# Sliding-window attention followed by a gated feed-forward: engine orders from a list scheduler on a model of the chip, PSUM banks given per stage, copies on either engine

## The chip, the cores and the metric

One core of a Trainium2 chip runs the whole program. The metric is device time in microseconds (us) of one execution. The kernel before takes 366.1 us. A comparison within 1% comes from runs in five rounds against the kernel before on the same chip.

Five engines run unsynchronized and in order, each its own list of instructions: TensorE (PE; PEld is its weight load), VectorE (DVE), ScalarE (ACT), GpSimd (POOL, which here issues the loads) and SyncE (SP, which issues the stores). They wait for one another by semaphores.

## The reference

Batch 8, 8 heads, sequence 576, head dimension 64. Attention with a causal window of 128 and a distance bias for each head, then a feed-forward over all 4608 tokens:

```python
scores = (q @ k.T) / 8 - slope[h] * abs(i - j)       # kept where 0 <= i - j < 128
attn   = exp(scores - max) / sum
x      = (attn @ v) transposed to (B*S, H*D)         # 4608 x 512
h      = x @ w_in                                    # 512 -> 2048, "GEMM 1"
g      = h * cos(h)
out    = g @ w_out                                   # 2048 -> 512, "GEMM 2"
```

## The kernel before

A small recorder keeps the instructions in the order in which the program is written, engine by engine, and derives the semaphore waits from what each operation reads and writes. So the order of every engine is the author's. PSUM is the memory that TensorE writes its results to; it is used here in eight banks. PSUM banks are keys such as `("B", 4)`: an operation that uses a bank waits for the one that used it last.

The feed-forward works in nine chunks of 512 tokens. Chunk `c` runs its GEMM 1 with the q/k transposes of batch `c+1` in between, then its GEMM 2 as filler between the pieces of attention `c+1`:

```python
def qk_transposes(banks, engs):         # 8 steps: pl in 0,1; q, k; columns (0,5) and (5,9)
    ...                                 # a step: 10 or 8 transposes into one bank, then
    ...                                 # one copy out, engs[n % 2] = "dve", "act"

def moe1(c, fc):                        # GEMM 1, one block of 128 hidden columns
    bank = HB[fc % 6]                   # banks 0..5
    ...                                 # 4 matmuls 128x512, cos on ACT, h*cos(h) on DVE

def moe2_steps(c):                      # GEMM 2: 4 outputs of 16 matmuls, banks 6 and 7
    ...                                 # copied out by DVE, stored by SP

def attention(b, fill, plan):           # units: ("t", None) = tail, then (pair, half)
    lead, part, last = plan
    take(lead)                          # lead matmuls of GEMM 2
    for j in range(2):
        scores(b, us[j], j); exps(b, us[j], j)
    mask(b, us[0])
    for j in range(n + 2):
        take(part[0] if j < n else last)
        if 2 <= j:      x_back(b, us[j - 2], j - 2, "act")
        if j + 2 < n:   scores(b, us[j + 2], j + 2); exps(b, us[j + 2], j + 2)
        if j < n:       take(part[1]); pv(b, us[j], j)
        if j + 1 < n:   mask(b, us[j + 1])
        if j < n:       norm(b, us[j], j)

for c in range(NCH):                    # ... c < 7:
    steps = iter(qk_transposes([6, 7], ["dve", "act"]))
    for fc in range(16):
        moe1(c, fc)
        if fc % 2 == 1:
            next(steps)()
    ...                                 # loads of batch c + 2
    attention(c + 1, moe2_steps(c), (8, (2, 3), 3))
```

A unit of attention is a pair of heads with one half of the first 512 positions; the tail is the last 64 positions, for all heads. PV is `attn @ v`. `take(n)` issues n filler matmuls of GEMM 2, and `x_back` transposes a finished unit into x.

TensorE uses its array in three ways. GEMMs, PV and most x transposes take it whole; the scores and the tail's x transposes use 64 rows at a time; the q/k transposes write 64 columns at a time. A change between these is called a tiling switch below.

The softmax here doesn't subtract the row's maximum and nothing guards it: scores larger than these inputs give would overflow.

Of the kernel before, what the change touches and what calls it, by code (L numbers as in the profile page):

```python
# [20 lines left out]
XA = 5 * CH  # L21
VW = 66


class Op:
    __slots__ = ("eng", "fn", "proc", "idx", "waits", "clock", "need", "val", "dma")


class Recorder:
# [3 lines left out]
    ENG = ("pe", "act", "dve", "pool", "sp")  # L33

    def __init__(self, nc, ctx):
        self.nc, self.ctx = nc, ctx
        self.handle = {"pe": nc.tensor, "act": nc.scalar, "dve": nc.vector,
                       "pool": nc.gpsimd, "sp": nc.sync}
        self.ops = {e: [] for e in self.ENG}
        self.writer, self.readers = {}, {}  # L40
        self.known = {e: {} for e in self.ENG}
        self.count = {}
        self.last = {}
        self.byproc = {}

    def _need(self, deps, d):
        if d is None:
            return
        cur = deps.get(d.proc)
        if cur is None or cur.idx < d.idx:  # L50
            deps[d.proc] = d

    def op(self, eng, fn, r=(), w=(), dma=None):
        o = Op()
        o.eng, o.fn, o.dma, o.need = eng, fn, dma, False
        raw, order = {}, {}
        for k in r:
            self._need(raw, self.writer.get(k))
        for k in w:
            self._need(order, self.writer.get(k))  # L60
            for d in self.readers.get(k, {}).values():
                if d.proc != eng or eng == "pool":
                    self._need(order, d)
        if dma is not None:
            self._need(order, self.last.get(("dma", dma)))
        known = self.known[eng]
        deps = dict(raw)
        for d in order.values():
            if d.proc == eng and eng == "pe":
                continue  # L70
            self._need(deps, d)
        if eng == "pe":
            deps.pop("pe", None)
        o.waits = []
        for p, d in sorted(deps.items(), key=lambda kv: str(kv[0])):
            if known.get(p, -1) >= d.idx:
                continue
            d.need = True
            o.waits.append(d)
        for d in o.waits:  # L80
            for p, i in d.clock.items():
                if known.get(p, -1) < i:
                    known[p] = i
            if known.get(d.proc, -1) < d.idx:
                known[d.proc] = d.idx
        o.proc = ("dma", dma) if dma is not None else eng
        o.idx = self.count.get(o.proc, 0)
        self.count[o.proc] = o.idx + 1
        o.clock = dict(known)
        self.last[o.proc] = o  # L90
        self.byproc.setdefault(o.proc, []).append(o)
        self.ops[eng].append(o)
        for k in r:
            self.readers.setdefault(k, {})[o.proc] = o
        for k in w:
            self.writer[k] = o
            self.readers[k] = {}
        return o

    def finish(self, final=()):  # L100
        nc, ctx = self.nc, self.ctx
        sems = {}
        for p, ops in self.byproc.items():
            name = p if isinstance(p, str) else f"d_{p[1]}"
            sems[p] = ctx.enter_context(nc.semaphore(f"s_{name}"))
            n = 0
            for o in ops:
                if o.dma is not None:
                    n += 16 * (len(o.fn) if isinstance(o.fn, list) else 1)
                elif o.need:  # L110
                    n += 1
                o.val = n
        block = ctx.enter_context(nc.Block())

        def run(e):
            h = self.handle[e]
            for o in self.ops[e]:
                for d in o.waits:
                    h.wait_ge(sems[d.proc], d.val)
                if o.dma is not None:  # L120
                    for f in (o.fn if isinstance(o.fn, list) else [o.fn]):
                        f(h).then_inc(sems[o.proc], 16)
                else:
                    ins = o.fn(h)
                    if o.need:
                        ins.then_inc(sems[e], 1)
            if e == "sp":
                for p in final:
                    h.wait_ge(sems[p], self.byproc[p][-1].val)
# [21 lines left out]

def bass_alibi_sliding__then__act_gcu_kernel(
# [8 lines left out]
    with ExitStack() as ctx:  # L161
# [3 lines left out]
        R = Recorder(nc, ctx)  # L165
# [12 lines left out]
        NP = 3  # L178
# [15 lines left out]
        HB = [0, 1, 2, 3, 4, 5]  # L194
# [12 lines left out]
        def load_qk(which, src, b):  # L207
            fns = []
            for g in range(2):
                fns.append(lambda e, g=g: e.dma_start(  # L210
                    qB[which][64 * g:64 * g + 64, :, :],
                    src[b, 4 * g:4 * g + 4, :, :].rearrange("h (s j) d -> s h (j d)", j=9)))
            op("pool", fns, w=[("qB", which)], dma=f"ld{which}")

        def load_v(b, order=range(NBLK)):
            for t in order:
                rows = 128 if t < 4 else 64
                op("pool", lambda e, t=t, rows=rows: e.dma_start(  # L218
                    vp[b % 2][0:rows, t, :, 0:64],
                    v[b, :, 128 * t:128 * t + rows, :].rearrange("h p d -> p h d")),  # L220
                   r=[("vinit", b % 2)], w=[("v", b % 2, t)], dma=f"ldv{b % 2}{t}")

        def load_w_in(u):
            op("pool", lambda e: e.dma_start(
                w_in[:, :, 512 * u:512 * u + 512],
                moe_w_in[:, 512 * u:512 * u + 512].rearrange("(k p) c -> p k c", p=128)),
               w=[("wi", u)], dma=f"wi{u}")

        def load_w_out(u):
            op("pool", lambda e: e.dma_start(  # L230
                w_out[:, 4 * u:4 * u + 4, :],
                moe_w_out[512 * u:512 * u + 512, :].rearrange("(f p) j -> p f j", p=128)),
               w=[("wo", u)], dma=f"wo{u}")


        def constants():
# [4 lines left out]
               w=["dif"] + sel)  # L241
            op("pool", lambda e: e.affine_select(
                dif[:, 0, :], dif[:, 0, :], pattern=[[-1, 128]], compare_op=ALU.is_ge,
                fill=-1.0e6, base=-1, channel_multiplier=1), r=["dif"], w=["dif"] + sel)
            op("pool", lambda e: e.affine_select(
                dif[:, 1, :], dif[:, 1, :], pattern=[[1, 128]], compare_op=ALU.is_ge,
                fill=-1.0e6, base=0, channel_multiplier=-1), r=["dif"], w=["dif"] + sel)
# [13 lines left out]
        def masks():  # L261
            for h in range(H):
# [3 lines left out]
                    ACTF.Exp, scale=slopes[h]), r=["dif"], w=[("EM", h)])  # L266
            for x in range(2):
# [3 lines left out]
                   r=[("EM", h) for h in range(x, H, 2)], w=["EMt"])  # L271


        def qk_transposes(banks, engs):

            out_ = []
            n = 0
            for pl in range(2):
                for which in ("q", "k"):
                    for (j0, j1) in ((0, 5), (5, 9)):  # L280
                        def step(pl=pl, which=which, j0=j0, j1=j1, n=n):
                            bank = banks[n % len(banks)]
                            nj = j1 - j0
                            dst = ps[:, bank, :].bitcast(BF16)[:, 0:nj * 128]

                            def tp(e):
                                ins = None
                                for j in range(j0, j1):
                                    for x in range(2):
                                        ins = e.transpose(  # L290
                                            dst[64 * x:64 * x + 64,
                                                128 * (j - j0):128 * (j - j0) + 128],
                                            qB[which][:, 2 * pl + x, 64 * j:64 * j + 64],
                                            ident[:, :])
                                return ins
                            op("pe", tp, r=[("qB", which), "ident"], w=[("B", bank)])
                            o = tr[which][:, :].rearrange("p (g l t) -> p g l t", g=2, l=2)[
                                :, :, pl, 0:576].rearrange("p g (s j) -> p g s j", j=9)[
                                :, :, :, j0:j1]
                            i = dst.rearrange("p (j g s) -> p g s j", j=nj, g=2)  # L300
                            key = ("tr", which, pl, j0)
                            if engs[n % len(engs)] == "act":
                                op("act", lambda e: e.activation(o, i, ACTF.Copy),  # L303
                                   w=[("B", bank), key])
                            else:
                                op("dve", lambda e: e.tensor_copy(o, i), w=[("B", bank), key])  # L306
                        out_.append(step)
                        n += 1
            return out_
# [7 lines left out]
        def units(b):  # L317
            if b == 0:
                return [(pr, G) for G in range(2) for pr in (0, 2, 1, 3)] + [("t", None)]
            return [("t", None)] + [(pr, G) for pr in range(NPAIR) for G in range(2)]  # L320

        def scores(b, u, n):
            slot = n % 2
            banks = [2 * slot, 2 * slot + 1]

            def f(e):
                ins = None
                if u[0] == "t":
# [314 lines left out]
```

## Time and profile before

| | before |
|---|---|
| time, median | 366.1 us |
| span of the profiled run | 365.3 us |
| TensorE busy | 93% |
| tiling switches on TensorE, in the order | 241 |
| length of a steady stage (one chunk and one attention) | 39.13 us |

From the page of the kernel before: busy time by engine; then the span in 40 slices, where each digit is the busy share, or the granted share of TensorE's clock, in tenths; then the chain of work that ended last, by engine.

```profile
PE 341.4 (93%) x2912; PEld 164.6 (45%) x2912; DVE 233.1 (64%) x446; ACT 234.5 (64%) x352; POOL 61.3 (17%) x89
PE   0688999999999999999999999999999999999996
PEclk9955999999999999999999999999999999999999
PE 79%; ACT 10%; DVE 6%; DMA 2%; issue 1%; POOL 1%; ACTq 0%; DVEq 0%; POOLq 0%
```

TensorE is nearly always busy from the fourth slice on, and the other engines have a third of their time free. But "busy" hides things: the time shown for a matmul is its latency (380 ns on average for L528), and matmuls overlap (they start 216 ns apart). The starts tell more. The timeline of TensorE, first two lines of the head, then part of one stage (start us, us from first start to last end, engine, line, operation, tiles, shapes, how many):

```profile
8.76 1.17 PE L290 MATMUL ps<-ident,qrows 128*64 128x128 bf16 x18 [8.76 <-DMA qrows<-in_q_dram]
...
30.62 3.57 PE L505 MATMUL ps<-xT,w_inb 128*128 128x512 bf16 x8 [0.24 <-ACT xT L487]
...
150.04 1.89 PE L505 MATMUL ps<-xT,w_inb 128*128 128x512 bf16 x8
151.86 0.47 PE L290 MATMUL ps<-ident,qrows 128*64 128x128 bf16 x10
152.26 1.90 PE L505 MATMUL ps<-xT,w_inb 128*128 128x512 bf16 x8
154.09 0.41 PE L290 MATMUL ps<-ident,qrows 128*64 128x128 bf16 x8
...
169.50 0.41 PE L333 MATMUL ps<-qt,kt 64*128 64x64 bf16 x16
169.74 0.33 PE L342 MATMUL ps<-qt,kt 64*128 64x256 bf16 x4
170.00 0.60 PE L528 MATMUL ps<-w_outb,gT 128*128 128x512 bf16 x2
171.23 0.40 PE L342 MATMUL ps<-qt,kt 64*128 64x256 bf16 x6 [0.62 <-ACT ptail L357]
```

In the stage, eight GEMM matmuls (L505) start 216 ns apart, which is 1.73 us, yet the transposes after them come 1.82 us later: the tiling switch cost 93 ns. In the raw starts the gap is 216 ns from matmul to matmul, 309 ns from a matmul into the transposes, and 56 ns within transposes but 152 ns out of them. The last line shows the other loss: scores wait 0.62 us for the bank that the tail's exp reads. That exp stands behind a table load on ScalarE (1.28 us, which comes wherever ScalarE changes between cos and exp). Of the waits of the whole run, three lines (who waited for what: us in total, times, longest):

```profile
PE ps L290 <- DMA qrows<-in_q_dram: 8.8, 1, 8.8
PE ps L342 <- ACT ptail L357: 4.4, 7, 0.6
PE ps L414 <- DVE rec L443: 0.8, 5, 0.2
```

The first is the start of the program, the second the wait just seen, once in each of seven stages.

### The profile page before, as it was taken

To read this page: it belongs to the slowest core of one execution; us is meant where nothing else is said; L and a number is where in the kernel's file an instruction comes from. 1 tells how busy PE (TensorE), PEld (TensorE's weight loads), DVE (VectorE), ACT (ScalarE), POOL (GpSimd) and SP (SyncE) were. 2 spreads that over 40 slices of the span, in tenths; PEclk is the share of its full clock that TensorE was granted. 3 is DMA by queue.
4 is the path that set the end of the run, shared out by engine and by line. 5 is a ranking of instruction groups with operands and counts; after the bars stand their busy time and mean duration, and the time that the engine had idled before them with its cause. 6 is when DMAs were issued, how large, how long until landed. Compare 5 with 4: busy or idle time off the path is not lost.

```text
span 365.3 us, 7057 instructions
## 1 busy us (share of the span) xinstructions
PE 341.4 (93%) x2912; PEld 164.6 (45%) x2912; DVE 233.1 (64%) x446; ACT 234.5 (64%) x352; POOL 61.3 (17%) x89
## 2 busy tenths in 40 slices
PE   0688999999999999999999999999999999999996
PEld 0453445544454445444544455444544454444442
DVE  1683767577666766675857676776657675754431
ACT  5684786577757786678657875777567765843400
POOL 8860051003400150006000420015000000000000
PEclk9955999999999999999999999999999999999999
DMA  7999979105910193109910691039110011001012
GB/s 114 183 207 206 142 107 125 54 29 66 158 59 31 22 160 75 57 2 135 118 59 0 82 144 58 31 51 160 47 55 0 0 59 60 0 4 56 29 59 86
DMA packets 55648, 28.25 MB, mean 77 GB/s; under 512 B 38720, under 2 KB 51008, under 8 KB 55616
## 3 DMA queue, kind: packets, MB, share of 16 engines
q0 software_dynamic: 50432, 18.36, 44.8%
q1 hardware_dynamic: 5184, 9.44, 6.9%
q8 instruction: 23, 0.38, 0.4%
q14 instruction: 9, 0.07, 0.1%
HBM read 36.70 MB, written 9.44 MB: 126 GB/s over the span
## 4 chain that ended last, share of the span: by engine, by line
PE 79%; ACT 10%; DVE 6%; DMA 2%; issue 1%; POOL 1%; ACTq 0%; DVEq 0%; POOLq 0%
PE ps L505 33%; PE ps L528 30%; PE ps L290 5%; PE ps L342 5%; ACT cos L511 3%; ACT L357 2%; DMA krows<-in_k_dram 2%; PE ps L414 2%; ACT ptail L357 2%; PE ps L473 2%; PE ps L417 1%; ACT kt L303 1%; DVE kt L306 1%; DVE ob L533 1%; DVE gT L514 1%; DVE p L380 1%
## 5 line engine op out<-in xcount | busy, mean ns | idle before, releaser
L528 PE MATMUL ps<-w_outb,gT 128*128 128x512 bf16 x576 | 151.4, 380 | 0.0
L505 PE MATMUL ps<-xT,w_inb 128*128 128x512 bf16 x576 | 138.5, 384 | 0.2 <-ACT xT L487 0.2
L511 ACT ACTIVATE cos<-ps,halfpi 128x512 f32<-128x512 f32 x144 | 98.9, 688 | 52.2 <-PE ps L505 47.7
L514 DVE TENSOR_TENSOR gT<-ps,cos 128x512 bf16<-128x512 f32 x144 | 99.5, 692 | 50.7 <-ACT cos L511 50.7
L505 PEld LDWEIGHTS ps<-xT,w_inb 128*128 128x128 bf16 x576 | 52.6, 98 | 62.2 <-issue 2.4
L528 PEld LDWEIGHTS ps<-w_outb,gT 128*128 128x128 bf16 x576 | 45.6, 97 | 39.6 <-issue 4.4
L366 ACT ACTIVATE p<-ps 128x768 bf16<-128x768 f32 (+1 forms) x64 | 57.6, 915 | 6.2 <-PE ps L342 6.2
L487 ACT ACTIVATE xT<-ps 128x256 bf16<-128x256 bf16 (+3 forms) x80 | 28.9, 363 | 48.5 <-PE ps L473 42.8
L533 DVE COPY ob<-ps 128x512 f32<-128x512 f32 x36 | 24.9, 691 | 34.4 <-PE ps L528 34.4
L380 DVE TENSOR_TENSOR p<-p,emask 128x768 bf16<-128x768 bf16 (+1 forms) x64 | 39.5, 616 | 1.1 <-ACT p L366 0.9
L210 POOL DMA_DIRECT2D qrows<-in_q_dram x16 | 10.1, 640 | 172.4 <-PE ps L290 171.6
L218 POOL DMA_DIRECT2D vp<-in_v_dram x40 | 34.0, 888 | 0.0
L342 PE MATMUL ps<-qt,kt 64*128 64x128 bf16 (+1 forms) x320 | 24.6, 248 | 5.4 <-ACT ptail L357 4.4
L444 DVE TENSOR_TENSOR xnat<-ps,rec 128x256 bf16<-128x256 f32 x64 | 27.2, 425 | 2.2
L414 PEld LDWEIGHTS ps<-vp,p 128*128 128x128 bf16 x256 | 18.3, 100 | 17.4 <-ACT xT L487 8.4
L414 PE MATMUL ps<-vp,p 128*128 128x65 bf16 x256 | 23.1, 198 | 2.2 <-DVE rec L443 0.8
L290 PE MATMUL ps<-ident,qrows 128*64 128x128 bf16 x288 | 15.0, 239 | 8.8 <-DMA qrows<-in_q_dram 8.8
L417 PE MATMUL ps<-vp,p 128*128 128x65 bf16 x192 | 21.1, 198 | 0.0
L473 PE MATMUL ps<-ident,xnat 128*128 128x128 bf16 x128 | 18.6, 230 | 1.4 <-DVE xtail L435 1.2
L290 PEld LDWEIGHTS ps<-ident,qrows 128*64 128x64 bf16 x288 | 10.0, 119 | 21.0 <-issue 12.3
L473 PEld LDWEIGHTS ps<-ident,xnat 128*128 128x128 bf16 x128 | 12.3, 101 | 14.9 <-DVE xtail L435 1.4
L342 PEld LDWEIGHTS ps<-qt,kt 64*128 64x128 bf16 x320 | 11.4, 96 | 16.4 <-ACT ptail L357 7.8
(42 smaller groups left out, 196.7 us busy)
## 6 DMA issues: line engine op xcount, KB each, us to landing
out_dram<-ob SPq DMA_DIRECT2D x36, 256.0 KB, 2.0
qrows<-in_q_dram POOLq DMA_DIRECT2D x16, 288.0 KB, 5.0
krows<-in_k_dram POOLq DMA_DIRECT2D x16, 288.0 KB, 5.1
vp<-in_v_dram POOLq DMA_DIRECT2D x32, 128.0 KB, 6.3
w_inb<-in_moe_w_in_dram POOLq DMA_DIRECT2D x4, 512.0 KB, 10.6
w_outb<-in_moe_w_out_dram POOLq DMA_DIRECT2D x4, 512.0 KB, 19.9
vp<-in_v_dram POOLq DMA_DIRECT2D x8, 64.0 KB, 5.7
```

Source lines behind the costliest of these rows:

```text
L218: op("pool", lambda e, t=t, rows=rows: e.dma_start(vp[b % 2][0:rows, t, :, 0:64], v[b, :, 128 * t:128 * t + rows, :].rearrange("h p d -> p ...
L290: ins = e.transpose(dst[64 * x:64 * x + 64, 128 * (j - j0):128 * (j - j0) + 128], qB[which][:, 2 * pl + x, 64 * j:64 * j + 64], ident[:, :])
L342: ins = e.matmul(ps[:, banks[x], c0:c1], keys_ap(x, pr, kc), query_ap(x, pr, qb, 128 * nb), start=True, stop=True)
L366: op("act", lambda e: e.activation(P[i][:, :, lo:512], ps[:, 2 * slot:2 * slot + 2, lo:512], ACTF.Exp, scale=0.125), w=[("B", 2 * slot), ( ...
L380: op("dve", lambda e: e.tensor_tensor(P[i][:, :, lo:512], P[i][:, :, lo:512], EM[:, 2 * pr:2 * pr + 2, lo:512], ALU.mult), r=[("P", i), (" ...
L414: ins = e.matmul(o, P[i][:, x, d0:d0 + 128], V[:, kc, h, 0:65], start=True, stop=not two)
L473: ins = e.transpose(dst[:, 128 * r:128 * r + 128], xnat[n % NX][:, 128 * r:128 * r + 128], ident[:, :])
L487: op("act", lambda e, o=o, i=i: e.activation(o, i, ACTF.Copy), w=[("B", bank)] + keys)
L505: ins = e.matmul(ps[:, bank, :], w_in[:, kc, 128 * fc:128 * fc + 128], xT[:, kc, r0:r0 + CH], start=(kc == 0), stop=(kc == NPAIR - 1))
L511: op("act", lambda e: e.activation(cosb[ci][:, :], ps[:, bank, :], ACTF.Sin, bias=halfpi[:, 0:1]), r=["halfpi"], w=[("B", bank), ("cos", ci)])
L514: op("dve", lambda e: e.tensor_tensor(gT[gi][:, fc, :], ps[:, bank, :], cosb[ci][:, :], ALU.mult), r=[("cos", ci)], w=[("B", bank), ("g", ...
L528: op("pe", lambda e: e.matmul(ps[:, bank, :], gT[gi][:, fc, 128 * t:128 * t + 128], w_out[:, fc, :], start=(fc == 0), stop=(fc == NFC - 1) ...
```

## The change

Its intent is to let a program decide the orders. Each operation now carries an estimate of how long it holds its engine, when its result is there, a priority, a tiling mode and (on ScalarE) a table phase. A list scheduler goes forward in model time, picks the next operation for each engine, and so fixes all five orders before anything is emitted. Copies out of PSUM may go to ScalarE or VectorE, whichever the scheduler finds free. Banks are assigned anew: GEMM 2 keeps banks 0 and 1 to itself (after the head), PV has 2 and 3, scores have 4 to 7, and GEMM 1 and the q/k transposes borrow from the last two groups. Loads of q and k are halved, transposes go 18 at a time, scores two units at a time. The exp results have four buffers instead of three. The arithmetic is the same.

```diff
+class Plan:
+    SWITCH = 95
+    TABLE = 1330
+    def op(self, eng, fn, r=(), w=(), dma=None, occ=100, lat=None, pri=5, mode=0, table=None):
 ...
+    def schedule(self):
 ...
+                    st = max(free[e], reach(o, e))
+                    if e == "pe" and o.mode != mode:
+                        st += self.SWITCH
+                    cand.append((st, o))
+                soon = min(st for st, _ in cand)
+                slack = 100 if e == "pe" else 40
+                st, o = min(((st, o) for st, o in cand if st <= soon + slack),
+                            key=lambda c: (c[1].pri, c[1].seq))
 ...
-        HB = [0, 1, 2, 3, 4, 5]
+        SB, UB, OB = [4, 5, 6, 7], [2, 3], [0, 1]
 ...
-                                op("dve", lambda e: e.tensor_copy(o, i), w=[("B", bank), key])
+                op(("act", "dve"),
+                   {"act": lambda e, o=o, i=i: e.activation(o, i, ACTF.Copy),
+                    "dve": lambda e, o=o, i=i: e.tensor_copy(o, i)},
+                   w=[("B", banks[n]), ("tr", which, pl, j0)],
+                   occ={"act": (730, 620)[n], "dve": (750, 620)[n]}, ...)
 ...
-        def scores(b, u, n):
+        def scores(b, us):                       # two units in one operation, mode=1
 ...
+                    for fc in range(NFC):
+                        if fc == 8:
+                            qk_transposes("q", 1, SB[0:2])
+                        if fc == 12:
+                            qk_transposes("k", 1, SB[0:2])
+                        moe1(c, fc, (UB + SB + UB + SB[2:] + UB + SB[2:] + UB)[fc])
```

## The prediction

> **What bounds the kernel now.** TensorE. The busy table has it at 341.4 of 365.3 us; VectorE and ScalarE are at 64%. The timeline repeats every 39.13 us for seven stages (chunk c's two GEMMs around attention c+1), with matmuls back to back. Starts of successive matmuls give the TensorE account: a 512-column matmul takes 216 ns, a 65-column one 29 to 30, a pair of tiled 128-column ones 56. Summed over all the work (estimate): 1152 x 0.216 = 248.8 us of GEMM, 16 of q/k transposes, 15 of scores, 17 of PV, 8 of x transposes, 305 us in all. The other 60 us: the head, tiling switches, waits, about 3.3 us of last copy and store.
>
> Each change between full, 64-row and 64-column use of the array widens the start gap by about 95 ns (216 to 310 into transposes, 56 to 152 out of them). The Trainium skill, "TensorEngine Tiling (Array Packing)", Key Properties, says a change of tiling mode drains the array; the trace agrees, at 95 ns. The instruction order has 241 such changes, 32 in a steady stage: 3.0 us. Waits cost about 1 us more a stage, mostly scores held behind the table load and the tail exp.
>
> **What the change does.** No arithmetic goes. The order shows 152 switches instead of 241, 20 in a steady stage: q/k transposes run 18 at a time, scores by twos. That is 12 x 0.095 = 1.1 us a stage; with the head, 89 x 0.095 = 8.5 us. After the tail scores 15 GEMM-2 matmuls (3.2 us) stand before the next thing that needs the exp, so the 0.62 us wait should go: about 4 us over the run, if new waits stay near 0.4 us a stage. Copies on either engine and bank changes free engines that do not bound, worth nothing directly.
>
> **Head.** Before, GEMM 1 starts at 30.6 us, at half clock until 35.7. Afterwards loads come in halves, so transposes start near 6 us instead of 8.8, exps finish near 21 to 22 instead of 25.7, and 8 GEMM-1 matmuls go early. But then the order puts the transposes of batch 1's q and k, and those loads land at 28.5 and 31.4 us in the trace of before, behind w_in on a saturated queue. The change doesn't shorten that queue. So I expect TensorE to stall until about 28 us and be dense from there, again cold for some microseconds: the head gives about 4 us, not the 9 that an earlier attention would suggest. ("TensorE: Matmul & The Clock Gate", Part 1: the clock is halved after idling and released by sustained work; the trace agrees, 0.5 from 18.5 to 35.7 us.)
>
> **The last part** (two GEMMs without attention, 55 us) is dense already: nothing.
>
> Sum: 8.5 + 4 + 4 = about 16 us. Predicted 350 us, range 344 to 356. Faster by over 2%: 0.93; within 2%: 0.06; slower: 0.01.
>
> **What shows it right.** Steady stage near 37.3 us; gaps at tiling changes still near 95 ns, but 20 a stage; "scores waited for tail exp" gone from the waits; first-batch transposes before 7 us; a TensorE wait for q or k of batch 1 ending near 28 us; TensorE busy sum little changed.
>
> **What makes it wrong.** The fixed order comes from a model: where it underestimates a latency (loads, exp-mask-PV chains, two banks for PV), TensorE waits in order and the saving is eaten; 0.5 us a stage is 3.5 us. If batch-1 loads land later, the head gains nothing. If w_in or GEMM 1 can fill the wait, the head gains up to 9 us. Two engines taking the copies may lengthen chains.

## The result, and the profile after

| | before | after |
|---|---|---|
| time, median | 366.12 us | 353.37 us (352.31 to 354.38, 4 runs) |
| ratio | | 0.9654 (95%: 0.9618 to 0.9689) |
| span of the profiled run | 365.3 us | 351.4 us |
| switches in the order | 241 | 152 |
| steady stage | 39.13 us | 37.3 us (only the last two of seven, see below) |

All outputs are right. The time fell by 12.75 us. It lies within the stated range of 344 to 356, 3.4 us above the point.

The same three parts of the page of the changed kernel:

```profile
PE 334.0 (95%) x2912; PEld 167.2 (48%) x2912; DVE 206.2 (59%) x451; ACT 236.2 (67%) x347; POOL 79.8 (23%) x121
PE   2768999999999999999999999999999999999996
PEclk9998999999999999999999999999999999999999
PE 90%; ACT 3%; DVE 2%; POOL 2%; DMA 1%; issue 1%; POOLq 0%; ACTq 0%
```

TensorE's share of the last chain rises from 79% to 90%; ScalarE's falls from 10% to 3%. The clock row shows half speed (5) in two slices before and in none after, where one half-speed stretch of 3.4 us (26.4 to 29.8 us) makes the 8. The 9s at the very start are no full speed: the clock record begins only at 14.6 us before and at 23.0 us after, and 18 transposes take 1.17 us at 5.97 us but 0.69 us at 31.47 us. The timeline of TensorE, changed kernel: first the head, then part of a steady stage.

```profile
5.97 1.17 PE L375 MATMUL ps<-ident,qrows 128*64 128x128 bf16 x18 [5.97 <-POOL ident L339]
...
27.79 1.90 PE L597 MATMUL ps<-xT,w_inb 128*128 128x512 bf16 x4
29.48 0.42 PE L569 MATMUL ps<-ident,xnat 128*128 128x128 bf16 x2
30.46 0.19 PE L491 MATMUL ps<-vp,ptail 128*128 128x65 bf16 x1 [0.57 <-ACT xT L583]
...
30.95 0.59 PE L597 MATMUL ps<-xT,w_inb 128*128 128x512 bf16 x2
31.47 0.69 PE L375 MATMUL ps<-ident,qrows 128*64 128x128 bf16 x18
...
182.81 0.59 PE L617 MATMUL ps<-w_outb,gT 128*128 128x512 bf16 x2
183.34 0.41 PE L415 MATMUL ps<-qt,kt 64*128 64x64 bf16 x16
183.58 0.33 PE L425 MATMUL ps<-qt,kt 64*128 64x256 bf16 x4
183.84 2.33 PE L617 MATMUL ps<-w_outb,gT 128*128 128x512 bf16 x10
```

Three things are to be seen. The first transposes start at 5.97 us instead of 8.76. In spite of that the first attention is not over until about 31 us, as before (its tail PV is at 30.46; the last x copy before ends at 30.8). And behind the tail's scores there now stand many GEMM-2 matmuls, so the wait for the tail's exp is gone. Of the waits of the changed kernel, four lines:

```profile
PE ps L375 <- POOL ident L339: 6.0, 1, 6.0
PE ps L569 <- DVE xnat L539: 2.7, 4, 0.8
PE ps L491 <- DVE ptail L463: 0.9, 4, 0.4
PEld ps L597 <- DVE gT L606: 7.3, 16, 0.5
```

The line "scores wait for the tail's exp" is not there any more. The 2.7 us of the x transposes (L569) lie in the head. Two new lines are: the tail PV (L491) waits a little for its mask, and the weight load of GEMM 1 (L597) waits for a bank that VectorE still reads. Most of those 7.3 us of the weight load overlap matmuls; in the starts they cost 2.1 us.

From the starts I made an account of TensorE. Each gap between starts is split into the time the earlier matmul needs (216 ns for 512 columns, 29 for 65, 56 for a tiled pair), up to 95 ns if the tiling changes, and the rest, called a wait if over 25 ns. From 31 us on:

| from 31 us to the last matmul's start | before | after |
|---|---|---|
| switches, us (number) | 21.2 (224) | 13.3 (141) |
| waits of scores, PV, GEMM 1 for other engines, us | 7.1 | 5.4 |
| GEMM-1 matmuls already done at 31 us | 1 | 7 |
| GEMM-1 matmuls that still run at half clock | about 8, at 427 ns | none |

The last matmul starts at 361.6 us before and at 347.8 us after, 13.8 us earlier.

### The profile page after: what moved, and what is told of

Its sections match the earlier page's. It is cut to its first block, busy times and chain, and to the rows that moved or that the text cites. A ratio compares the mean times of both kernels' runs of the same rounds, so it can differ in the third digit from the quotient of the medians.

```text
span 351.4 us, 7156 instructions
## 1 busy us (share of the span) xinstructions
PE 334.0 (95%) x2912; PEld 167.2 (48%) x2912; DVE 206.2 (59%) x451; ACT 236.2 (67%) x347; POOL 79.8 (23%) x121
## 4 chain that ended last, share of the span: by engine, by line
PE 90%; ACT 3%; DVE 2%; POOL 2%; DMA 1%; issue 1%; POOLq 0%; ACTq 0%
PE ps L597 37%; PE ps L617 33%; PE ps L375 5%; PE ps L425 5%; PE ps L505 3%; PE ps L569 2%; PE ps L508 2%; DMA krows<-in_k_dram 1%; ACT ptail L447 1%; DVE ptail L463 1%; PE ps L491 1%; ACT L447 1%; POOL qrows L298 1%; PE ps L415 1%; PE ps L493 1%
## 5 line engine op out<-in xcount | busy, mean ns | idle before, releaser
L617 PE MATMUL ps<-w_outb,gT 128*128 128x512 bf16 x576 | 138.7, 379 | 0.0
L597 PE MATMUL ps<-xT,w_inb 128*128 128x512 bf16 x576 | 137.7, 382 | 0.0
L606 DVE TENSOR_TENSOR gT<-ps,cos 128x512 bf16<-128x512 f32 x144 | 92.1, 686 | 70.5 <-PE ps L617 55.9
L602 ACT ACTIVATE cos<-ps,halfpi 128x512 f32<-128x512 f32 x144 | 93.2, 689 | 29.0 <-PE ps L617 13.4
L597 PEld LDWEIGHTS ps<-xT,w_inb 128*128 128x128 bf16 x576 | 52.2, 98 | 62.8 <-DVE gT L606 7.3
L617 PEld LDWEIGHTS ps<-w_outb,gT 128*128 128x128 bf16 x576 | 53.9, 98 | 58.7 <-issue 2.2
L298 POOL DMA_DIRECT2D qrows<-in_q_dram x32 | 19.8, 634 | 129.3 <-PE ps L375 61.6
L623 ACT ACTIVATE ob<-ps 128x512 f32<-128x512 f32 x31 | 18.5, 597 | 44.7 <-PE ps L617 44.7
L539 DVE TENSOR_TENSOR xnat<-ps,rec 128x256 bf16<-128x256 f32 x64 | 26.4, 418 | 0.5
L298 POOL DMA_DIRECT2D krows<-in_k_dram x32 | 19.6, 636 | 8.5 <-PE ps L597 7.5
L569 PE MATMUL ps<-ident,xnat 128*128 128x128 bf16 x128 | 18.5, 229 | 2.7 <-DVE xnat L539 2.7
L583 ACT ACTIVATE xT<-ps 128x256 bf16<-128x256 bf16 (+3 forms) x36 | 12.6, 353 | 12.0 <-PE ps L569 11.8
L386 ACT ACTIVATE kt<-ps 128x640 bf16<-128x640 bf16 (+1 forms) x21 | 15.8, 777 | 4.3 <-PE ps L375 4.3
L537 DVE RECIPROCAL rec<-ps 128x4 f32<-128x4 f32 x64 | 11.2, 178 | 8.7 <-PE ps L508 7.3
## 6 DMA issues: line engine op xcount, KB each, us to landing
w_outb<-in_moe_w_out_dram POOLq DMA_DIRECT2D x4, 512.0 KB, 18.5
```

What stands on the lines that cost most here:

```text
L298: fns.append(lambda e, g=g: e.dma_start(qB[which][64 * g:64 * g + 64, 2 * pl:2 * pl + 2, :], src[b, 4 * g + 2 * pl:4 * g + 2 * pl + 2, :, ...
L597: op("pe", lambda e, kc=kc: e.matmul(ps[:, bank, :], w_in[:, kc, 128 * fc:128 * fc + 128], xT[:, kc, r0:r0 + CH], start=(kc == 0), stop=(k ...
L602: op("act", lambda e: e.activation(cosb[ci][:, :], ps[:, bank, :], ACTF.Sin, bias=halfpi[:, 0:1]), r=["halfpi"], w=[("B", bank), ("cos", c ...
L606: op("dve", lambda e: e.tensor_tensor(gT[gi][:, fc, :], ps[:, bank, :], cosb[ci][:, :], ALU.mult), r=[("cos", ci)], w=[("B", bank), ("g", ...
L617: op("pe", lambda e, t=t, fc=fc, bank=bank: e.matmul(ps[:, bank, :], gT[gi][:, fc, 128 * t:128 * t + 128], w_out[:, fc, :], start=(fc == 0 ...
```

## The experiments

The theories. **Theory 1:** TensorE bounds the kernel; each tiling switch costs it about 95 ns, and fewer switches are most of the gain, with filled waits second. **Rival:** the scheduler's filled waits and the freer engines earn the gain, and switches are paid for elsewhere. **Theory 2** (after the result): the head's gain was lost in the chain of the first attention. Medians of the kernel before in these rounds were 365.4 to 366.3 us. In the diffs, lines in plain words stand for longer code.

### One part alone, in the old order: transposes 18 at a time (b_pairs)

```diff
-    step: 10 or 8 transposes into one bank of [6, 7], one copy
+    step: 18 transposes into banks 6 and 7, one copy on DVE and one on ACT
-        if fc % 2 == 1:
+        if fc % 4 == 3:
             next(steps)()
```

> The kernel before with one part of the change alone: q/k transposes 18 at a time instead of 10 and 8, everything else in the old order. The order has 185 tiling switches instead of 241. Theory 1 (each switch costs about 95 ns of TensorE time and most of the gain is switches): 52 of those 56 switches lie in the dense part, so 4.9 to 5.3 us less, about 361 us. Rival (the gain comes from filled waits and freer engines; the 95 ns are hidden elsewhere): within 1 us of before. A third outcome: two banks taken at once make the next transposes or GEMM 1 wait, and part of the 5 us comes back as waits.

Measured: 371.0 us, ratio 1.0143: 5.2 us slower, with 56 switches fewer. The third outcome came about. The waits of this kernel (GEMM 2 is L531 here), and the place in its timeline:

```profile
PE ps L531 <- DVE kt L308: 12.2, 7, 2.0
...
129.15 0.82 DVE L308 COPY kt<-ps 128x640 bf16<-128x640 bf16 x1
130.02 1.90 PE L531 MATMUL ps<-w_outb,gT 128*128 128x512 bf16 x8 [1.70 <-DVE kt L308]
```

The last group of transposes takes both of GEMM 2's banks, so GEMM 2 waits up to 2 us for the copy. That is 12.2 us in seven stages, more than the switches saved.

### The same, with the groups earlier (b_pairs_early)

```diff
-        if fc % 4 == 3:
+        if fc % 3 == 1 and fc < 12:
             next(steps)()
```

> As b_pairs (the kernel before, transposes 18 at a time, 185 switches), but the four groups stand after GEMM-1 blocks 1, 4, 7 and 10 instead of 3, 7, 11 and 15. b_pairs lost 12.2 us to seven waits of GEMM 2 for the last copy out of bank 6, because the last pair takes both of GEMM 2's banks just before GEMM 2 starts. Theory 1 (95 ns a switch, plus a bank wait that hid it): the bank wait goes and 5 us of switches stay saved, about 361 us. Rival (in a fixed hand order grouping does not pay, whatever the banks): 365 us or more.

Measured: 358.8 us, ratio 0.9794: 7.5 us faster than before. No wait of GEMM 2 for the copy is left; what remains in the stages is mainly

```profile
PE ps L345 <- ACT ptail L360: 3.0, 7, 0.4
```

3.0 us of the old wait of scores (4.4 us before). By the account, switches from 31 us on cost 15.9 us instead of 21.2, which is 5.3 us for 56, or 94 ns each. So theory 1 holds for the cost of a switch. It also shows that a hand order reaches 7.5 of the 12.75 us with one part of the change, if the banks allow it. Of the other 2.2 us, 1.4 are the shorter wait of scores, which was not expected: the last q/k copy on ScalarE no longer stands between the last cos and the table load, so the tail's exp comes sooner against TensorE. The rest lies in the head, where full speed came at 33.6 us instead of 35.1 in the profiled runs; that changes from run to run.

### Filling the one large wait by hand (b_lead11)

```diff
-                attention(c + 1, moe2_steps(c), (8, (2, 3), 3))
+                attention(c + 1, moe2_steps(c), (11, (2, 3), 3))
```

> The kernel before with 11 instead of 8 GEMM-2 matmuls ahead of the tail scores, and three fewer at the end of the stage. In the trace of before TensorE waits 0.69 us in each of seven stages for the tail exp behind the table load, and 3 matmuls are 0.65 us. Theory 1 with the wait term of the prediction: 4 to 4.8 us less, about 362 us. Rival (the wait only moves to the next dependent thing, because ScalarE's chain through table load, exp, mask sets the pace): less than 1.5 us less.

Measured: 368.2 us, ratio 1.0066: 2.4 us slower. Theory 1's outcome failed, and the rival's came about: the wait moved. The timeline shows how:

```profile
130.87 0.41 PE L333 MATMUL ps<-qt,kt 64*128 64x64 bf16 x16
131.32 1.02 ACT L357 ACTIVATE ptail<-ps 128x1024 bf16<-128x1024 f32 x1 [0.46 <-PE ps L333]
...
132.40 0.39 PE L342 MATMUL ps<-qt,kt 64*128 64x256 bf16 x6 [0.42 <-ACT ptail L357]
133.66 0.69 DVE L533 COPY ob<-ps 128x512 f32<-128x512 f32 x1 [0.58 <-PE ps L528]
...
135.97 0.25 PE L414 MATMUL ps<-vp,p 128*128 128x65 bf16 x3 [0.48 <-DVE xtail L435]
```

The three matmuls stand ahead of the tail's scores, so the exp now waits for the scores (0.46 us), and 0.42 of the 0.62 us remain. And an output tile is complete three matmuls sooner, so its copy on VectorE falls ahead of the mask and the normalization that PV waits for (0.48 us). The filler was put on the wrong side of the producer, and the in-order VectorE passed the shift on.

### The changed kernel with the old number of switches (a_ungrouped)

```diff
-    SWITCH = 95
+    SWITCH = 0
     q/k transposes: two operations of 10 and 8 instead of one of 18
     scores: one operation for each unit instead of one for two
```

> The changed kernel with its list scheduling, banks and either-engine copies kept, but transposes again in 10 and 8, scores one unit at a time, and the price of a switch in the scheduler set to 0. The order has 239 switches, as good as before's 241, against 152. Theory 1: 87 x 0.095 = 8.3 us slower than the changed kernel, of which a few may fall into waits: about 360 to 362 us, so only about 4 to 6 us better than before. Rival (list scheduling's filled waits and freer engines earn the gain): 353 to 356 us.

Measured: 362.2 us, ratio 0.9896 to before. The changed kernel has 0.9654, so 0.0242 of 366 us, 8.9 us, went with the grouping; 8.3 us were expected. A second, stricter count of the starts gives it 5.3 us of waits from 31 us on against 4.9 in the changed kernel, so the loss is not in waits. What is left of the gain without the grouping, 3.8 us, is the scheduler's order, the head, the banks and the fourth buffer; no run took the last two alone.

### Copies on the engines of before (a_fixed_engines)

```diff
-    op(("act", "dve"), {"act": ..., "dve": ...}, ...)        # x, output and q/k copies
+    op("act", ...)   # x;   op("dve", ...)   # outputs;   q/k halves: dve, act
```

> The changed kernel with each copy out of PSUM back on the engine that it had before (x copies on ScalarE, output copies on VectorE, q/k halves on VectorE and ScalarE), scheduled anew; 153 switches. Theory 1: TensorE bounds and the other two engines have room, so within 1.5 us of the changed kernel, 352 to 355 us. Rival (either engine shortens the chains TensorE waits for): 3 us or more slower, 356 us or more.

Measured: 352.8 us, ratio 0.9642, the same as the changed kernel. Either-engine copies are worth nothing here.

### The head: mask exps first (a_emask)

```diff
-    ACTF.Exp, scale=slopes[h]), r=["dif"], w=[("EM", h)], occ=520, lat=612, table=0)
+    ACTF.Exp, scale=slopes[h]), r=["dif"], w=[("EM", h)], occ=520, lat=612, table=0, pri=0)
```

In the changed kernel ScalarE builds some mask factors late, in the middle of the first attention:

```profile
18.16 1.66 ACT L353 ACTIVATE emask<-dif 128x512 bf16<-128x512 f32 x3
20.57 0.81 ACT L455 ACTIVATE p<-ps 128x768 bf16<-128x768 f32 x1 [0.75 <-PE ps L508]
```

A mask multiplication needs them, PV needs the mask, and the next exp needs the buffer that PV frees.

> The changed kernel with one priority changed: the eight exps that build the mask factors go first on ScalarE instead of filling gaps; 153 switches. In the trace after, three of them run at 18.2 to 19.8 us, a mask multiplication waits for the last, and the first attention ends at 31 us though it began 4.7 us earlier than before. Theory 2 (the head's gain was lost to this chain): attention 0 ends 2 to 3 us earlier, TensorE is dense from about 29 us, when batch 1's q lands at 28.7, and the time falls by 1.5 to 2.5 us, to about 351.4. Rival (the loads of batch 1, as my prediction had it, or the half clock bound the head): under 0.7 us.

Measured: 352.0 us, ratio 0.9606 against 0.9654, about 1.8 us faster than the changed kernel by the ratios (1.4 by the medians). In its trace:

```profile
28.41 0.26 PE L491 MATMUL ps<-vp,ptail 128*128 128x65 bf16 x1
...
31.65 0.69 PE L375 MATMUL ps<-ident,qrows 128*64 128x128 bf16 x18
```

The tail PV comes 2.05 us sooner than in the changed kernel (30.46), and 9 instead of 7 GEMM-1 matmuls are done by 31 us. So theory 2 holds in direction, and the size fits. The intervals of the two ratios just overlap, and the two kernels were not timed side by side, so the size is not sharp.

### Corrected costs (a_tuned), and the head known to the model (a_best)

```diff
-    TABLE = 1330
+    TABLE = 1420
-    tail's x transposes: mode 0;   tail's mask: lat=693
+    tail's x transposes: mode 1;   tail's mask: lat=860
 # a_best, in addition:
+    land = {"ldq0": [5800, 28700], "ldk0": [7900, 30100], ...}      # measured landings, ns
+    if e == "pe" and st < 23000:
+        o.occ, o.lat = 2 * o.occ, o.lat + o.occ
```

The planned starts can be laid beside the measured ones, operation by operation. The plan of the changed kernel was already 6 us too early at 39 us and slipped 4 more in the rest; 1.3 us of that at the tail PV and 1.4 us at the tail's x transposes, whose tiling the plan had wrong.

> The changed kernel with the scheduler told what the trace shows: the tail's x transposes are in the 64-row mode, the table switch costs 1.42 us instead of 1.33, the tail's mask result reaches TensorE 0.17 us later. 143 switches instead of 152. Comparing planned with measured starts, the steady stages slip 1.3 us at the tail PV and 1.4 us at the tail x transposes over the run. Theory 1 (switches and waits behind the table load are what is left): about 2 us faster, 351.4 us. Rival (a new order only moves the waits): within 0.7 us of 353.4.

> a_tuned with a scheduler that also knows the head: measured landing times of the first loads, engines' real start, TensorE at half rate until 23 us; mask exps then fall into ScalarE's early gaps. 144 switches. Theories 1 and 2 together: a_tuned's and a_emask's gains add, about 349 to 350 us. If the head is bound by batch 1's loads, no better than a_tuned.

Measured: a_tuned 352.6 us (0.9622), 0.8 us below the changed kernel, between the two outcomes (2 us, or within 0.7): the tail PV's wait shrank from 1.6 to 0.4 us in the account, but new small waits came (total 5.5 us as against 5.4). a_best 351.0 us (0.9582), 1 us short of the 349 to 350 expected. The gains of the head and the tail are small, about as large together as they were apart.

### Fewer switches still (a_slack, a_best_slack)

The line that decides how eagerly a more urgent operation breaks in has a constant of 100 ns, just above the price of a switch:

```diff
-                slack = 100 if e == "pe" else 40
+                slack = 10 if e == "pe" else 40
```

> The changed kernel with one number changed in the scheduler: on TensorE a more urgent operation may be preferred only if it can start within 10 ns of the soonest one, not within 100. With 100 a tiling switch (priced 95) was always accepted, and 15 planned idle gaps of 80 ns stand in the plan (measured 156 ns each, 2.1 us). The order has 97 switches instead of 152. Theory 1 (95 ns a switch, TensorE bounds): 55 x 0.095 = 5.2 us plus up to 2 us of waits, about 346 to 349 us. Rival (attention's chain is now served later, so exps and masks come late and TensorE waits): 352 us or more.

> a_best with the same 10 ns, 101 switches instead of 144. Theories 1 and 2: 43 x 0.095 = 4.1 us plus up to 2 us of waits below a_best's 351.0, about 345 to 347.5 us; the rival as for a_slack: 350 us or more.

Measured: 425.7 us (ratio 1.1644) and 423.9 us (1.161). Both expectations failed by over 75 us, though the orders have only 97 and 101 switches. The page of a_slack, its waits, and its timeline:

```profile
PE   3579986999598995999589995999589986999996
PEclk9999995799859995799859995799859995799999
PE ps L425 <- ACT p L455: 23.4, 16, 2.4
...
95.36 13.11 PE L617 MATMUL ps<-w_outb,gT 128*128 128x512 bf16 x60
108.40 0.69 PE L375 MATMUL ps<-ident,qrows 128*64 128x128 bf16 x18
...
114.62 0.93 PE L425 MATMUL ps<-qt,kt 64*128 64x256 bf16 x10 [2.39 <-ACT p L455]
117.38 0.93 PE L425 MATMUL ps<-qt,kt 64*128 64x256 bf16 x10 [0.83 <-ACT p L455]
```

With 10 ns a switch is never taken while work of the same tiling is at hand. So 60 GEMM-2 matmuls run in a row (13 us), and when attention's turn comes there is no filler left for its chain of scores, exp, mask, PV. TensorE waits there in every stage, and its clock halves as well (the 5s and 7s; 13.65 us in each of seven stages). How the 72 us divide between waiting and the half clock was not separated. The rival was right, and the model had foreseen it: run without the chip, the scheduler in this run's kernel.py plans an end at 414 us, and that of the changed kernel at 341 us (measured spans 425.1 and 351.4). The expectation made no use of it. What the order must keep is filler between the links of the chain, and the switches are the price of it.

### The same rule without the harm (a_best_gap, a_gap)

```diff
-                    if e == "pe" and o.mode != mode:
-                        st += self.SWITCH
-                    cand.append((st, o))
-                soon = min(st for st, _ in cand)
-                slack = 100 if e == "pe" else 40
-                st, o = min(((st, o) for st, o in cand if st <= soon + slack), ...)
+                    turn = self.SWITCH if e == "pe" and o.mode != mode else 0
+                    cand.append((st + turn, st, o))
+                soon = min(bare for _, bare, _ in cand)
+                slack = 30 if e == "pe" else 40
+                st, o = min(((st, o) for st, bare, o in cand if bare <= soon + slack), ...)
```

> a_best in which TensorE's tiling switch no longer counts in the comparison of start times (so urgent attention work may always break in, as with 100 ns) but an idle gap of at most 30 ns may be taken for a more urgent operation. 139 switches. It separates the two things that the 10 ns did in a_slack. Theory 3 (a_slack lost 72 us because attention was served last, not because of the gaps): this run is as fast as a_best or up to 2.5 us faster (the 2.2 us of waits of GEMM 1 for a bank go), 348.5 to 351 us. If forbidding the gaps itself did the harm: 355 us or more.

> The changed kernel with the rule of a_best_gap alone (switches left out of the comparison, gaps of at most 30 ns), without the corrections to the head and the tail. 150 switches against 152. If the rule itself earns the 6.2 us between a_best and a_best_gap: about 347 us. If it earned them only with the corrected head (attention 0 ending early, clock kept up): 350 to 352 us, the 2.1 us of bank waits and little else.

Measured: a_best_gap 344.8 us (ratio 0.9423), 6.2 us below a_best where at most 2.5 us were expected; it is the fastest of all, 21.2 us below before. a_gap, the rule alone in the changed kernel, 349.35 us (0.956), 3.4 us below it by the ratios, 4.0 by the medians, between the two outcomes named. So forbidding the gaps did no harm, and theory 3 holds: a_slack's loss was the starved chain. The rule alone earns 3.4 to 4 us; the other 2 us or so came only together with the corrected head and tail. In the head of a_best_gap:

```profile
26.50 0.59 PE L608 MATMUL ps<-xT,w_inb 128*128 128x512 bf16 x2
27.71 0.81 PE L608 MATMUL ps<-xT,w_inb 128*128 128x512 bf16 x3
28.70 0.69 PE L385 MATMUL ps<-ident,qrows 128*64 128x128 bf16 x18 [0.18 <-DMA qrows<-in_q_dram]
```

Attention 0 is nearly done by 28 us, and now TensorE does wait for batch 1's q, as the prediction had it for the changed kernel. Most of the gain of the rule is waits of TensorE. By the second count, those from 31 us on fall from 4.9 us in the changed kernel (5.4 by the account above) to 1.1 in a_gap, and from 3.7 us in a_best to 0.4 in a_best_gap. In that last trace 50 of the 2912 matmul records are missing; they show as gaps that are one matmul, 216 ns, too long, and were left out. How the other half of the 6.2 us divides between head, switches and clock stays open.

## Why the prediction was right or wrong

- **TensorE bounds the kernel: right.** It has 79% of the last chain before and 90% after. Moving the copies between the other engines changed nothing (352.8 against 353.4 us).
- **The cost of a switch: right.** Predicted 89 x 0.095 = 8.5 us. The account gives 22.7 us of switches before and 14.3 after over the whole run, 8.4 us. Taking the grouping back cost 8.9 us. Where the starts could be read, a switch added 93 to 96 ns in both kernels.
- **Waits: right in kind, wrong in size.** The prediction named the table-load wait (gone) and expected 4 us, "if new waits stay near 0.4 us a stage". New waits cost 5.4 us from 31 us on where 7 x 0.4 = 2.8 were allowed for; 2.1 us of them are GEMM 1 behind a bank and 1.6 us the tail PV. So 7.1 us became 5.4, a gain of 1.7 us, not 4. These 2.3 us are most of the miss of 3.4 us.
- **Head: near in size (about 3.4 us in the profiled runs, 4 predicted) by luck: two errors cancel.** The failed step is "I expect TensorE to stall until about 28 us and be dense from there, again cold for some microseconds". There was no wait for batch 1's loads: q landed at 28.7 us, but TensorE came to it at 31.47, because the first attention, begun 4.7 us earlier, still ended at about 31 us: its last exp ended at 25.5 us (25.7 before), where the prediction had "21 to 22". Its chain was stretched by late mask factors (shown by a_emask) and by a cold TensorE and loads that the plan had too early (argued from the trace; a_best changed these together). Against that, the clock was at full speed from 29.8 us on, where before it was half from 18.0 until 35.1 us (the prediction read 18.5 and 35.7, and called what came before it idling: TensorE was busy for 2.0 of the 3.4 us before 18.0), and six more GEMM-1 matmuls were done by 31 us: about 2.1 and 1.3 us. Part of the 2.1 us is chance: of the 49 runs of the kernel before in the experiments' rounds, the 12 with a mean clock of 0.977, as in the profiled run, average 366.7 us, the other 37 average 365.7. "TensorE: Matmul & The Clock Gate", Part 1, of the Trainium skill says the clock is released after a busy window of about 3.4 us; in the kernel before it took 4.5 us of nearly gapless work, from 30.6 to 35.1 us.
- **The last part: nearly right.** After the last attention no gap between GEMM matmuls is over 216 ns before; in the changed kernel six of the new bank waits lie there, 0.156 us each, 0.9 us in all.
- **The steady stage: right in two of seven.** Predicted 37.3 us. From one tail exp to the next the changed kernel takes 25.6, 31.7, 33.8, 31.7, 37.9, 37.33 and 37.36 us (before: 28.2, then about 39.1 each). The scheduler lets attention run ahead and puts GEMM work off: after the last attention 73 us are left, against 56 before. So this number tests little; the account of the whole run tests more.
- **Sum.** From 31 us on, switches give 7.9 us (21.2 less 13.3) and waits 1.7; with a head of about 3.4 us these make 13.0 of the 13.8 us by which the last matmul came earlier. The other 0.8 us is not assigned. The medians differ by 12.75 us; the profiled run of before, at 367.24 us, was 1.1 us above its median.

## What to carry to other kernels

When one engine is busy nine tenths of the time, make an account of it from the starts of its instructions: needed time, mode switches, waits. Each entry can be priced before the change, but a saving in an in-order engine is only kept if the banks and the neighbours' queues allow it: the same grouping cost 5 us in one place and earned 7.5 us a few blocks earlier. Minimizing the priced thing alone is a trap: the order with the fewest switches was 72 us slower, because the filler that hides a dependent chain was spent before the chain began; and where a scheduler plans from a model, read its planned end before the run, lay planned starts beside measured ones and look first at its tie-breaking constants.

## What the Trainium skill lacked or had wrong

- "TensorEngine Tiling (Array Packing)", Key Properties, says that a change of tiling mode drains the array, but gives no cost. The runs show 93 to 96 ns for each change, in both directions, and 94 ns each from the 56 changes that b_pairs_early saved.
- "ScalarE: Activation LUTs", What ACT_TABLE_LOAD costs, gives 1283 ns for the load and about 2.66 us with a drain for each switch of set. The load is 1.28 us in these traces, but between the end of a cos (48.69 us) and the start of the exp (50.00 us) of the changed kernel there are 1.31 us in all, and 1.31 to 1.36 us at each of its 15 changes of set: no further drain shows.
- No page has a number for what a gain on an in-order engine loses through a shared PSUM bank: b_pairs paid 12.2 us of waits for 5.3 us of switches saved.
